# One buffer per slot: the scheduler's choice of a slot carried into the program

## Chip, cores, metric

The kernel runs on one core of a Trainium2 chip. The metric is the device time of one execution in microseconds (us), here the median of three runs. Beside it stands one profiled execution, from which every row below is taken.

## What is computed

The reference is an attention over 32 learned memory slots followed by two feed-forward layers, all in fp32 (8 batches, 8 heads, 576 tokens of 64; 4608 tokens of 512 in the layers, inner width 2048):

```python
a = softmax(phi, over the sequence)
k_m = einsum('bhsm,bhsd->bhmd', a, k);  v_m = einsum('bhsm,bhsd->bhmd', a, v)
attn = softmax(q @ k_m.T / sqrt(64))
x = (attn @ v_m), heads side by side          # 4608 x 512
h = relu(x @ w_in);  x = (s * h * h + b) @ w_out
h = x @ w1;          out = (h * sigmoid(1.702 * h)) @ w2
```

## The kernel before

The work has four stages, each bound to TensorE (PE). In the first, eight batches go through the attention, and `v_m` is multiplied into `w_in`, so that one product gives `h`. The other three are the products with `w_out`, `w1` and `w2` (called `wo`, `w1`, `w2`), each in 6 blocks of 768 tokens. These three use the scheme of Strassen's kind with sums and differences of quarter matrices (tiles named A, B, C, D, E, r). Each fp32 operand is split into a high part `oh` and a low part `ol` (`od` holds both parts of a half tile): ScalarE (ACT) or VectorE (DVE) casts the high part (`hi`, line 276 or 277) and DVE subtracts it (`lo`, line 282). Three matmuls then stand for one product: high by weight-high, low by weight-high, high by weight-low (lines 1217, 1218, 1219 in the last stage). Results in PSUM (X, Y, Z) leave by copies on ACT (`u`, `c`, `a`, line 1236) and additions on DVE. Tiles of the intermediate results lie in HBM and are loaded by transfers that SyncE (SP) issues (line 266).

In the last stage some products of one block belong to another block's output as well. Their sum leaves PSUM as a tile `z` (ACT, line 1346 or 1343), and GpSimd (POOL) issues a transfer that adds it to the output in HBM (`onto`, line 271). The tile's place in SBUF stays taken until that transfer has landed.

The program order of every engine comes from a scheduler written in Python, the class `Order`. Each operation is handed to it with a due time, the tiles it reads and writes, and a cost for each engine that could do it; `sort()` then plays the operations through in modelled time. A tile takes a slot of its tag (`BUFS`: 30 for "w", 33 for "t", 4 for PSUM "ps", 2 for "km", 4 for "nm" and "sm"). The scheduler keeps, for each tag, a heap `free` of the modelled times at which its slots come free, gives a new tile the earliest of them, and puts a slot back at the end of its last user plus 0.2. In that model an engine's result counts as done a little after its operation, a transfer by SP 3.0 after it, and an adding transfer 8.0 after it:

```python
END_LAG = {"sync": 3.0, "acc": 8.0, "dve": 0.09, "act": 0.09}
```

What `sort()` hands on is the order of operations only. When the program is then written in that order, `Net.t` asks a pool of the framework for each tile, with the tag and its number of slots; the pool gives one of the tag's slots whose users all stand earlier in the program, and the first instruction on the new tile waits until the last of those users has ended, or, for a transfer, has landed.

Of the kernel before, what the change touches and what calls it, by code (L numbers as in the profile page):

```python
# [27 lines left out]
class Order:  # L28
# [15 lines left out]
    def __init__(self, bufs):  # L44
        self.bufs, self.ops, self.rank, self.fill, self.until, self.since = bufs, [], [], None, 0, 0
        self.narrow = set()
        self.wrote, self.read, self.users = {}, {}, {}

    def add(self, due, ways, r=(), w=(), first=0):
# [19 lines left out]
    def sort(self):  # L69
        ops, rank = self.ops, self.rank  # L70
        left = [len(o[2]) for o in ops]
        after = [[] for _ in ops]
        tiles = {}
        for n, (due, _, deps, new) in enumerate(ops):
            for d in deps:
                after[d].append(n)
            for x in new:
                tiles.setdefault(x[0], []).append((due, n, x))
        queue = {tag: [x for _, _, x in sorted(v, key=lambda e: e[:2])] for tag, v in tiles.items()}
        free = {tag: [0.0] * n for tag, n in self.bufs.items()}  # L80
        uses = {x: len(v) for x, v in self.users.items()}
        last = dict.fromkeys(uses, 0.0)
        at, end, on, out = {}, [0.0] * len(ops), [None] * len(ops), []
        of = [[] for _ in ops]
        for x, v in self.users.items():
            for n in v:
                of[n].append(x)
        run = False
        held = {"dve": 0.0, "pool": 0.0}
        ready = sorted((rank[n], n) for n in range(len(ops)) if not left[n])  # L90
        since = {n: 0.0 for _, n in ready}
        while ready:
            can = {}
            limit = ready[0][0] + self.AHEAD
            for due, n in ready:
                if due > limit and can:
                    break
                _, ways, deps, new = ops[n]
                t0 = 0.0
                if new:  # L100
                    ok = True
                    for tag in {x[0] for x in new}:
                        mine = [x for x in new if x[0] == tag]
                        f = free[tag]
                        if len(f) < len(mine) or any(x not in queue[tag][:len(f)] for x in mine):
                            ok = False
                            break
                        t0 = max(t0, f[0] if len(mine) == 1 else heapq.nsmallest(len(mine), f)[-1])
                    if not ok:
                        continue  # L110
                best = None
                for i, (eng, cost, _, port) in enumerate(ways):
                    t = max(t0, at.get(eng, 0.0))
                    if port:
                        t = max(t, held["dve" if eng == "pool" else "pool"])
                    for d in deps:
                        e = end[d] + (self.LAG[eng] if on[d] != eng else 0.05)
                        if e > t:
                            t = e
                    score = t + cost * self.WEIGHT.get(eng, 1.0)  # L120
                    if best is None or score < best[0]:
                        best = score, t, eng, i
                can.setdefault(best[2], []).append((best[1], due, n, best[3]))
            if not can:
                raise RuntimeError("no order")
            first = []
            for tag, v in can.items():
                t0 = min(v)[0]
                like = [c for c in v if c[0] <= t0 + 0.1 and c[2] in self.narrow and c[1] >= self.since] if tag == "pe" and run else ()
                if like:  # L130
                    c = min(like, key=lambda c: c[1:])
                    if c[1] < min(v, key=lambda c: c[1:])[1] + self.NEAR:
                        first.append(c)
                        continue
                first.append(min((c for c in v if c[0] <= t0 + (self.SLACK if c[1] < self.until else 0.0)), key=lambda c: c[1:]))
            t, _, n, i = min(first)
            _, ways, _, new = ops[n]
            eng, cost, fn, port = ways[i]
            if port:
                held[eng] = t + cost  # L140
            if self.fill and eng == "pe":
                out.append(lambda n=int((t - at.get(eng, 0.0)) * self.FILL): self.fill and self.fill(n))
            for x in new:
                queue[x[0]].remove(x)
                heapq.heappop(free[x[0]])
            at[eng], on[n] = t + cost, eng
            end[n] = t + cost + self.END_LAG.get(eng, 0.0)
            ready.remove((rank[n], n))
            if eng == "pe":
                run = n in self.narrow  # L150
            out.append(fn)
            for m in after[n]:
                left[m] -= 1
                if not left[m]:
                    bisect.insort(ready, (rank[m], m))
            for x in of[n]:
                last[x] = max(last[x], end[n])
                uses[x] -= 1
                if not uses[x]:
                    heapq.heappush(free[x[0]], last[x] + 0.2)  # L160
        self.span = max(end)
        self.end, self.on = end, on
        return out


class Net:
# [50 lines left out]
    def t(self, k, shape, dt=F32):  # L217

        self.n += 1
        pool = self.ps if k[0] == "ps" else self.sb  # L220
        x = pool.tile(shape, dt, tag=k[0], bufs=self.BUFS[k[0]], name=f"{self.name(k)}_{self.n}")
        self.T[k] = x
        return x

# [1313 lines left out]
```

## Time and profile before

| | |
|---|---|
| time, median of 3 runs | 1376.75 us (1376.53 to 1376.81) |
| the profiled execution, its time | 1375.49 us |
| its span, first to last instruction | 1373.7 us |
| mean granted TensorE clock, as a share of full speed | 0.991 |
| PE busy, share of the span | 1342.7 us, 98% |
| DVE busy | 1130.5 us, 82% |
| ACT busy | 851.4 us, 62% |

An engine is busy while one of its instructions runs. "Idle before" an instruction is the time since the one before it on its engine ended, and the profile names the instruction or transfer whose end released it. An idle time with the releaser "issue" is one for which the profile shows no releaser. Of the profiled execution 1.8 us lie outside the span.

### The profile page before, as it was taken

What the parts mean: (1) busy time and instruction counts of PE and PEld (TensorE: products, weight loads), DVE (VectorE), ACT (ScalarE), POOL (GpSimd) and SP (SyncE); (2) the same over time, 40 slices, a digit from 0 to 9 for tenths busy, and PEclk for the clock granted to TensorE, in tenths of its full rate; (3) what the DMA queues carried; (4) which work ended last, traced back from release to release, by engine and by line L of the source; (5) the groups of instructions that cost most, each with busy time, mean ns of one, the idle gap of its engine ahead of it and who ended that gap; (6) DMA issues with size and microseconds to landing.
All of it is one profiled execution on the core that took longest, in us unless ns stands there. A gap on an engine that the chain in (4) does not pass through costs nothing.

```text
span 1373.7 us, 24220 instructions
## 1 busy us (share of the span) xinstructions
PE 1342.7 (98%) x9088; PEld 1296.6 (94%) x9088; DVE 1130.5 (82%) x1634; ACT 851.4 (62%) x1194; POOL 78.1 (6%) x71
## 2 busy tenths in 40 slices
PE   7999999999999999999999999999999998989898
PEld 6888888899999999999999999999999998989898
DVE  6878996998979988998885997784587786888785
ACT  5766666888877777886564765664454354544443
POOL 2201220200000000000000000000000010101011
PEclk8999999999999999999999999999999999999999
DMA  9989999797865765799999699799898574867673
GB/s 366 364 308 344 341 353 322 263 320 246 303 183 186 245 222 160 248 347 367 349 355 336 259 326 345 272 345 351 316 354 297 192 206 151 225 192 214 216 209 79
DMA packets 149766, 380.49 MB, mean 277 GB/s; under 512 B 16656, under 2 KB 27536, under 8 KB 149648
## 3 DMA queue, kind: packets, MB, share of 16 engines
q1 hardware_dynamic: 145472, 373.24, 77.4%
q0 software_dynamic: 4176, 5.70, 3.1%
q8 instruction: 71, 1.16, 0.4%
q14 instruction: 47, 0.39, 0.1%
HBM read 232.41 MB, written 146.47 MB: 276 GB/s over the span
## 4 chain that ended last, share of the span: by engine, by line
PE 83%; issue 6%; DVE 4%; DMA 4%; ACT 3%; POOL 0%; SPq 0%; ACTq 0%; DVEq 0%; POOLq 0%
PE X L935 5%; PE X L933 5%; PE X L934 5%; PE h L306 5%; PE X L1081 5%; PE X L1083 5%; PE X L1082 5%; PE h L308 4%; PE h L307 4%; PE X L1218 3%; PE X L1219 3%; PE X L1217 3%; PE Y L935 2%; PE Y L933 2%; PE Y L934 2%
## 5 line engine op out<-in xcount | busy, mean ns | idle before, releaser
L306 PE MATMUL h<-ah,mh 128*128 128x288 f32 x512 | 154.9, 302 | 0.3
L308 PE MATMUL h<-ah,ml 128*128 128x288 f32 x512 | 151.0, 295 | 0.2 <-ACT ml L816 0.2
L307 PE MATMUL h<-al,mh 128*128 128x288 f32 x512 | 150.8, 295 | 0.0
L282 DVE TENSOR_TENSOR ol<-A,oh 128x768 fp32r<-128x768 f32 x120 | 113.3, 954 | 33.7 <-ACT oh L276 18.2
L276 ACT CAST oh<-A 128x768 fp32r<-128x768 f32 x111 | 94.5, 866 | 72.7 <-issue 24.6
L1081 PE MATMUL X<-oh,w 128*128 128x384 f32 x384 | 128.6, 335 | 1.2 <-ACT u L1093 0.7
L935 PE MATMUL X<-oh,wo 128*128 128x384 f32 x384 | 128.3, 334 | 0.0
L934 PE MATMUL X<-ol,wo 128*128 128x384 f32 x384 | 128.3, 334 | 0.0
L1082 PE MATMUL X<-ol,w 128*128 128x384 f32 x384 | 128.3, 334 | 0.0
L1083 PE MATMUL X<-oh,w 128*128 128x384 f32 x384 | 128.3, 334 | 0.0
L933 PE MATMUL X<-oh,wo 128*128 128x384 f32 x384 | 128.3, 334 | 0.0
L835 ACT ACTIVATE r<-h 128x576 f32<-128x576 f32 x123 | 86.4, 705 | 59.5 <-PE h L308 50.1
L1217 PE MATMUL X<-oh,w 128*128 128x384 f32 x320 | 110.1, 344 | 8.1 <-ACT u L1236 4.9
L1219 PE MATMUL X<-oh,w 128*128 128x384 f32 x320 | 109.5, 342 | 0.0
L306 PEld LDWEIGHTS h<-ah,mh 128*128 128x128 f32 x512 | 96.1, 188 | 12.3 <-issue 4.5
L1218 PE MATMUL X<-ol,w 128*128 128x384 f32 x288 | 99.2, 344 | 5.4 <-DVE ol L282 5.4
L308 PEld LDWEIGHTS h<-ah,ml 128*128 128x128 f32 x512 | 96.1, 188 | 0.4 <-ACT ml L816 0.4
L307 PEld LDWEIGHTS h<-al,mh 128*128 128x128 f32 x512 | 96.1, 188 | 0.2
L276 ACT CAST oh<-B 128x768 fp32r<-128x768 f32 x70 | 58.9, 856 | 45.6 <-DVE ol L282 18.6
L271 POOL DMA_DIRECT2D out<-z x29 | 25.7, 992 | 1079.7 <-DVE z L282 913.1
L276 ACT CAST oh<-C 128x768 fp32r<-128x768 f32 x68 | 58.7, 879 | 34.7 <-DVE C L282 12.3
L282 DVE TENSOR_TENSOR ol<-B,oh 128x768 fp32r<-128x768 f32 x72 | 67.6, 953 | 12.3 <-DMA out<-z 8.7
(293 smaller groups left out, 3891.6 us busy)
## 6 DMA issues: line engine op xcount, KB each, us to landing
w<-w SPq DMA_DIRECT2D x132, 512.0 KB, 5.8
r<-r SPq DMA_DIRECT2D x128, 288.0 KB, 4.5
kv<-in_kv SPq DMA_DIRECT2D x72, 258.0 KB, 5.4
g<-u SPq DMA_DIRECT2D x48, 384.0 KB, 4.7
raw<-in_w SPq DMA_DIRECT2D x32, 512.0 KB, 6.1
q<-in_q SPq DMA_DIRECT2D x32, 288.0 KB, 5.5
A<-r SPq DMA_DIRECT2D x24, 384.0 KB, 4.8
B<-r SPq DMA_DIRECT2D x24, 384.0 KB, 4.9
```

The lines of the kernel that those rows point to most:

```text
L276: self.order.add(due, [self.act(n, lambda: nc.scalar.copy(out(), src()), psum), self.dve(n, lambda: nc.vector.tensor_copy(out(), src()), f ...
L282: self.order.add(due, [self.dve(n, lambda: nc.vector.tensor_tensor(out(), a(), b(), op=op), port=port)], r, w, first)
L306: self.nc.tensor.matmul(ps, wh, xh, start=start and i == 0, stop=False)
L307: self.nc.tensor.matmul(ps, wh, xl, start=False, stop=False)
L308: self.nc.tensor.matmul(ps, wl, xh, start=False, stop=(i == n - 1))
L933: nc.tensor.matmul(out, T[w][:, 0, c], T[h][:, p], start=f, stop=False, skip_group_check=True)
L934: nc.tensor.matmul(out, T[w][:, 0, c], T[l][:, p], start=False, stop=False, skip_group_check=True)
L935: nc.tensor.matmul(out, T[w][:, 1, c], T[h][:, p], start=False, stop=last, skip_group_check=True)
L1081: nc.tensor.matmul(out, T[w][:, 0, c], T[h][:, k], start=f, stop=False, skip_group_check=True)
L1082: nc.tensor.matmul(out, T[w][:, 0, c], T[l][:, k], start=False, stop=False, skip_group_check=True)
L1083: nc.tensor.matmul(out, T[w][:, 1, c], T[h][:, k], start=False, stop=k == 1, skip_group_check=True)
L1217: nc.tensor.matmul(out, T[w][:, 0, c], T[h][:, p], start=f, stop=False, skip_group_check=True)
```

## The change

The scheduler's heap now holds pairs of a time and the number of a slot. When a tile takes its slot, the number is kept in `slot`, and it goes back into the heap with the slot's next time. `Net.t` asks the pool no longer for "one of 33 slots of tag t" but for the only slot of a tag named after the letter and the number, "t17" say. So the slot that the scheduler chose is the one that the program uses.

```diff
--- before.py
+++ after.py
@@ -44,6 +44,7 @@
     def __init__(self, bufs):
         self.bufs, self.ops, self.rank, self.fill, self.until, self.since = bufs, [], [], None, 0, 0
         self.narrow = set()
+        self.slot = {}
         self.wrote, self.read, self.users = {}, {}, {}
 
     def add(self, due, ways, r=(), w=(), first=0):
@@ -77,7 +78,7 @@
             for x in new:
                 tiles.setdefault(x[0], []).append((due, n, x))
         queue = {tag: [x for _, _, x in sorted(v, key=lambda e: e[:2])] for tag, v in tiles.items()}
-        free = {tag: [0.0] * n for tag, n in self.bufs.items()}
+        free = {tag: [(0.0, i) for i in range(n)] for tag, n in self.bufs.items()}
         uses = {x: len(v) for x, v in self.users.items()}
         last = dict.fromkeys(uses, 0.0)
         at, end, on, out = {}, [0.0] * len(ops), [None] * len(ops), []
@@ -105,7 +106,7 @@
                         if len(f) < len(mine) or any(x not in queue[tag][:len(f)] for x in mine):
                             ok = False
                             break
-                        t0 = max(t0, f[0] if len(mine) == 1 else heapq.nsmallest(len(mine), f)[-1])
+                        t0 = max(t0, f[0][0] if len(mine) == 1 else heapq.nsmallest(len(mine), f)[-1][0])
                     if not ok:
                         continue
                 best = None
@@ -142,7 +143,7 @@
                 out.append(lambda n=int((t - at.get(eng, 0.0)) * self.FILL): self.fill and self.fill(n))
             for x in new:
                 queue[x[0]].remove(x)
-                heapq.heappop(free[x[0]])
+                self.slot[x] = heapq.heappop(free[x[0]])[1]
             at[eng], on[n] = t + cost, eng
             end[n] = t + cost + self.END_LAG.get(eng, 0.0)
             ready.remove((rank[n], n))
@@ -157,7 +158,7 @@
                 last[x] = max(last[x], end[n])
                 uses[x] -= 1
                 if not uses[x]:
-                    heapq.heappush(free[x[0]], last[x] + 0.2)
+                    heapq.heappush(free[x[0]], (last[x] + 0.2, self.slot[x]))
         self.span = max(end)
         self.end, self.on = end, on
         return out
@@ -218,7 +219,7 @@
 
         self.n += 1
         pool = self.ps if k[0] == "ps" else self.sb
-        x = pool.tile(shape, dt, tag=k[0], bufs=self.BUFS[k[0]], name=f"{self.name(k)}_{self.n}")
+        x = pool.tile(shape, dt, tag=f"{k[0]}{self.order.slot[k[:2]]}", bufs=1, name=f"{self.name(k)}_{self.n}")
         self.T[k] = x
         return x
```

The order of instructions is the same on all five engines, tile for tile (8064 rows of PE, 1636 of DVE, 1196 of ACT and 998 of SP). What differs is which earlier tile lay in a tile's slot, and with it the addresses and the waits: 1055 of the 2386 tiles follow another tile than before. Three places show it. In these rows the last number in a name is the tile's own, and behind each instruction stand the counters it waits for: `DMAHW` counts transfers issued from SP, `DMASW` those issued from POOL, `Activation`, `DVE` and `PE` count those engines' instructions.

The first place is ACT in the last stage, where the fourth block begins (z tiles 2023 and 2046 are copied out here). Before:

```order
L1346 COPY z2_2023_12750<-Z2_1894_11977 128x768 [waits PE_49]
L276 CAST oh_2029_12786<-B_1980_12526 128x768 [waits DVE_49,PE_49]
L276 CAST oh_2032_12798<-B_1984_12541 128x768 [waits DVE_49]
L1236 COPY u2_2033_12812<-X_1964_12413 128x768 [waits PE_49]
L276 CAST oh_2034_12815<-B_1993_12585 128x768
L276 CAST oh_2037_12837<-C_2022_12747 128x768 [waits DMAHW7_49,PE_49]
L276 CAST oh_2039_12846<-C_2026_12767 128x768 [waits DMAHW0_49,DVE_49]
L276 CAST oh_2042_12864<-C_2028_12772 128x768 [waits DMAHW1_49,PE_49]
L276 CAST oh_2043_12867<-C_2030_12791 128x768 [waits DMAHW4_49,DMAHW2_49]
L276 CAST oh_2045_12875<-A_2035_12821 128x768 [waits DMAHW3_49,PE_49]
L1346 COPY z2_2046_12890<-Z2_1894_11977 128x384 [waits PE_49]
L276 CAST oh_2052_12927<-A_2038_12840 128x768 [waits DMAHW4_49,DMASW6_49,Activation_49]
```

and after the change:

```order
L1347 COPY z2_2023_12750<-Z2_1894_11977 128x768 [waits DMASW3_49,DMASW2_49]
L277 CAST oh_2029_12786<-B_1980_12526 128x768 [waits DVE_49,PE_49,Activation_49]
L277 CAST oh_2032_12798<-B_1984_12541 128x768 [waits DVE_49,PE_49,Activation_49]
L1237 COPY u2_2033_12812<-X_1964_12413 128x768 [waits PE_49]
L277 CAST oh_2034_12815<-B_1993_12585 128x768 [waits DVE_49]
L277 CAST oh_2037_12837<-C_2022_12747 128x768 [waits DMAHW7_49,PE_49]
L277 CAST oh_2039_12846<-C_2026_12767 128x768 [waits DMAHW0_49,PE_49]
L277 CAST oh_2042_12864<-C_2028_12772 128x768 [waits DMAHW4_49,DMAHW1_49,PE_49]
L277 CAST oh_2043_12867<-C_2030_12791 128x768 [waits DMAHW2_49,DVE_49,Activation_49]
L277 CAST oh_2045_12875<-A_2035_12821 128x768 [waits DMAHW5_49,DMAHW3_49,PE_49]
L1347 COPY z2_2046_12890<-Z2_1894_11977 128x384 [waits DMASW5_49,DMASW4_49,PE_49]
L277 CAST oh_2052_12927<-A_2038_12840 128x768 [waits DMAHW4_49,PE_49]
```

The cast `oh_2052` waited for a transfer of POOL, because it took the slot of `z2_2046` (both lie at byte 128224 of a partition); now it lies where `ol_2031` was, and waits for PE, while `z2_2046` takes the slot of `z2_2023`. The cast `oh_2032` took the slot of `B_1980` before, whose last reader is the DVE instruction that writes `ol_2031`; now it takes that of `oh_2011`, which PE reads last.

The second place is DVE beside it, with the subtraction that writes `ol_2031`. Before:

```order
L282 TENSOR_TENSOR ol_2024_12752<-B_1993_12585,oh_2020_12730 128x768 [waits PE_49,Activation_49]
L282 TENSOR_TENSOR ol_2027_12769<-B_1977_12513,oh_2021_12745 128x768 [waits PE_49,Activation_49]
L282 TENSOR_TENSOR B_1993_12585<-D_2019_12728,A_1946_12290 128x768 [waits DMAHW6_49,DVE_49]
L282 TENSOR_TENSOR A_1930_12192<-C_2022_12747,A_1930_12192 128x768 [waits DMAHW7_49]
L282 TENSOR_TENSOR ol_2031_12796<-B_1980_12526,oh_2029_12786 128x768 [waits DMASW5_49,DMASW4_49,Activation_49]
L282 TENSOR_TENSOR A_1934_12213<-C_2026_12767,A_1934_12213 128x768 [waits DMAHW0_49]
```

and now:

```order
L283 TENSOR_TENSOR ol_2024_12752<-B_1993_12585,oh_2020_12730 128x768 [waits DMAHW5_49,Activation_49]
L283 TENSOR_TENSOR ol_2027_12769<-B_1977_12513,oh_2021_12745 128x768 [waits PE_49,Activation_49]
L283 TENSOR_TENSOR B_1993_12585<-D_2019_12728,A_1946_12290 128x768 [waits DMAHW6_49,DVE_49]
L283 TENSOR_TENSOR A_1930_12192<-C_2022_12747,A_1930_12192 128x768 [waits DMAHW7_49]
L283 TENSOR_TENSOR ol_2031_12796<-B_1980_12526,oh_2029_12786 128x768 [waits PE_49,Activation_49]
L283 TENSOR_TENSOR A_1934_12213<-C_2026_12767,A_1934_12213 128x768 [waits DMAHW0_49]
```

`ol_2031` took the slot of `z2_2023` before and now takes one that PE reads last (`ol_2013`); `ol_2024` now follows a tile that a transfer of SP stores.

The third place is SP at the same point of the program, with the loads of the next block's tiles A. Before:

```order
L266 DMA C_2028_12772<-g_2_2_1_0_9713 128x768 [waits DMAHW1_49,DVE_49]
L266 DMA C_2030_12791<-g_2_3_1_0_9868 128x768 [waits DMAHW2_49,PE_49]
L266 DMA A_2035_12821<-g_3_0_0_0_10036 128x768 [waits DMAHW3_49,PE_49]
L266 DMA A_2038_12840<-g_3_1_0_0_10174 128x768 [waits DMAHW4_49,PE_49]
L266 DMA A_2041_12862<-g_3_2_0_0_10305 128x768 [waits PE_49]
L266 DMA r3_2044_12873<-g_1_0_1_1_8713 128x768 [waits DMAHW6_49,DVE_49,Activation_49]
L266 DMA A_2048_12894<-g_3_3_0_0_10457 128x768 [waits DMAHW7_49,PE_49]
```

and now:

```order
L267 DMA C_2028_12772<-g_2_2_1_0_9713 128x768 [waits DMAHW1_49,DVE_49]
L267 DMA C_2030_12791<-g_2_3_1_0_9868 128x768 [waits DMAHW2_49,PE_49]
L267 DMA A_2035_12821<-g_3_0_0_0_10036 128x768 [waits DMAHW3_49,PE_49]
L267 DMA A_2038_12840<-g_3_1_0_0_10174 128x768 [waits DMAHW4_49,DVE_49]
L267 DMA A_2041_12862<-g_3_2_0_0_10305 128x768 [waits DMAHW5_49,PE_49]
L267 DMA r3_2044_12873<-g_1_0_1_1_8713 128x768 [waits DMAHW6_49,PE_49]
L267 DMA A_2048_12894<-g_3_3_0_0_10457 128x768 [waits DMAHW7_49,PE_49]
```

The load of `A_2038` waited for PE and now waits for DVE, since it takes the slot of `B_1984`, whose last reader is the subtraction that writes `ol_2036`. The loads behind it on SP start after it.

## Rows read from the trace of the kernel before

**Rows 1.** The page's part 1: busy time, share of the span, instructions.

```profile
span 1373.7 us, 24220 instructions
...
PE 1342.7 (98%) x9088; PEld 1296.6 (94%) x9088; DVE 1130.5 (82%) x1634; ACT 851.4 (62%) x1194; POOL 78.1 (6%) x71
```

**Rows 2.** Windows of the second and the last stage: length, busy time of each engine.

```profile
core 0: us, PE busy (x) PEld busy (x) DVE busy (x) ACT busy (x) POOL busy (x), PEclk, DMA share, GB/s
343.00:694.00 351.00, 351.00 (x2027) 351.00 (x2026) 316.43 (x422) 263.60 (x354) 0.00 (x0) 1.00 0.77 264
1030.00:1373.70 343.70, 323.34 (x1811) 319.04 (x1809) 265.51 (x353) 159.11 (x219) 25.71 (x29) 0.98 0.66 198
```

**Rows 3.** PE's waits: instruction and releaser; us in total, times, longest.

```profile
PE X L1218 <- DVE ol L282: 5.4, 5, 2.4
PE X L1217 <- ACT u L1236: 4.9, 2, 4.0
...
PE X L1081 <- ACT u L1093: 0.7, 1, 0.7
```

**Rows 4.** Windows of PE alone around its stalls and at the low clock.

```profile
1139.80:1156.00 16.20, 11.61 (x52) 0.89 0.51 155
1148.90:1152.30 3.40, 3.40 (x13) 0.50 0.98 274
1216.00:1220.20 4.20, 0.24 (x2) 1.00 0.01 4
1220.60:1224.00 3.40, 3.40 (x12) 0.50 0.51 200
1269.80:1279.70 9.90, 5.22 (x26) 0.94 0.87 273
1278.60:1285.40 6.80, 6.49 (x19) 0.50 0.15 40
1317.60:1345.00 27.40, 24.00 (x135) 1.00 0.54 150
```

**Rows 5.** ACT in order of time at the first stall: start, duration, [idle before].

```profile
1139.28 0.83 ACT L276 CAST oh<-B 128x768 fp32r<-128x768 f32 x1 [8.31 <-DVE ol L282]
1140.02 0.79 ACT L1236 COPY u<-X 128x768 f32<-128x768 f32 x1
...
1145.12 0.47 ACT L1346 COPY z<-Z 128x384 f32<-128x384 f32 x1
1153.80 1.56 ACT L276 CAST oh<-A 128x768 fp32r<-128x768 f32 x2 [8.21 <-issue]
```

**Rows 6.** DVE in order of time at the first stall.

```profile
1138.29 0.96 DVE L282 TENSOR_TENSOR ol<-B,oh 128x768 fp32r<-128x768 f32 x1 [4.49 <-DMA out<-z]
...
1140.90 0.95 DVE L282 TENSOR_TENSOR ol<-B,oh 128x768 fp32r<-128x768 f32 x1
```

**Rows 7.** ACT's waits over the whole span: us in total, times, longest.

```profile
ACT oh L276 <- issue: 24.6, 3, 8.3
```

**Rows 8.** Line 271, the adding transfers: who waited, and issue to landing.

```profile
  DVE ol L282: 13.0, 5
...
DMA to landing us min/median/max: 3.5/5.3/8.6
```

**Rows 9.** POOL in order of time at the first stall.

```profile
1145.94 0.86 POOL L271 DMA_DIRECT2D out<-z  x1 [13.59 <-ACT z L1346]
```

**Rows 10.** PE in order of time, two matmuls that release slots.

```profile
1131.25 0.33 PE L1219 MATMUL X<-oh,w 128*128 128x384 f32 x1
...
1200.01 0.33 PE L1218 MATMUL Y<-ol,w 128*128 128x384 f32 x1
```

**Rows 11.** SP's issues, ACT and DVE in order of time ahead of the second stall.

```profile
1203.07 0.32 SPq L266 DMA_DIRECT2D C<-g  x1
...
1212.39 0.96 DVE L282 TENSOR_TENSOR A<-C,A 128x768 f32<-128x768 f32 x1 [3.11 <-DMA C<-g]
...
1212.95 0.83 ACT L276 CAST oh<-A 128x768 fp32r<-128x768 f32 x1 [8.06 <-issue]
```

**Rows 12.** SP's issues at the first stall.

```profile
1133.02 4.11 SPq L266 DMA_DIRECT2D A<-g  x3
```

## The prediction

> **What bounds the kernel now.** I read the page's shares first: PE is busy for 98% of the span, and no other engine is above 82% [rows 1]. Then the windows by stage. The second stage has no idle PE at all, while in the last stage PE is busy for 323.34 of 343.70 us, so 20.36 us are idle there [rows 2]. Of these, 3.7 us lie behind the last matmul, and the change doesn't touch them; the rest is idle time between matmuls. Third, PE's waits: nearly all of it is the first matmul on an operand or on X, which waits for a low part from DVE or for a copy from ACT [rows 3]. Fourth, windows around these waits give the sizes by difference of length and busy time [rows 4]: 4.59 us at 1139.8 to 1156, 3.96 at 1216, 4.68 at 1269.8 to 1279.7, and 3.40 at 1317.6 to 1345, in all 16.63. Behind the first three of them the granted clock is 0.50 of full speed, the 1.2 GHz level instead of 2.4, for 3.40, 3.40 and 6.49 us of busy PE [rows 4]. At half speed that time does half the work, so it costs 6.65 us more. Behind the waits that add up to 3.40 the clock stays at 1.00. So stalls and their clock cost 23.3 us; the rest of the span is PE at full speed.
>
> **Why ACT and DVE are late there.** In the first stall a DVE subtraction `ol` stands idle for 4.49 us until an adding transfer `out<-z` has landed [rows 6]. Its inputs have nothing to do with z: it has the slot that z left. The next cast on ACT idles 8.31 us until that subtraction ends, because its slot is that of the tile read there, and the copy `u`, for which PE waits, stands right behind the cast in ACT's queue [rows 5]. Then ACT idles another 8.21 us, with no releaser named: the cast `oh<-A` at 1153.80. The order rows say what it is: this cast waits for a transfer of POOL, and it has the slot of the z copied at 1145.12 [rows 5], whose transfer POOL issued at 1145.94 [rows 9]; at the 8.6 us that the slowest of these takes to land [rows 8], 1154.5, at the 7.8 that the cast's start implies, 1153.7. Three casts on ACT idle this way for 24.6 us together [rows 7], and DVE idles 13.0 for the same transfers [rows 8]. The pool knew only that the instruction that issues the transfer stands earlier in the program.
>
> **The change, part by part.**
>
> *Instructions.* None is added, removed or moved on any engine, so no busy time changes; the term is 0. What changes is what a tile's first instruction waits for.
>
> *The z slots.* They now go to tiles that come much later. At the first stall `z` itself, at 1145.12 [rows 5], takes the slot whose transfer had landed before the subtraction at 1138.29 began [rows 6], 6.8 us before. Matching the addresses of the built program with the trace, the 17 tiles that follow a z start 5 to 13 us after its landing, where before 16 of 17 started as it landed. The cast of 1139.28 gets a slot whose last reader is the matmul of 1131.25, done at 1131.58 [rows 10]: it could run about 7.7 us earlier, and `u` right behind it, long before PE wants it at 1139.9.
>
> *First stall, 4.59 us.* `u` and both casts leave the path. Next late is the low part of the first tile A, which DVE reaches after the sums that wait for loads C. Those loads wait for DVE's earlier subtractions, which no longer stand behind z, so I take them 2 to 4 us earlier, where 1.9 is needed (the longest of the waits for a low part is 2.4 [rows 3]). Remainder 0.3, with bounds 0 and 1.6.
>
> *Second stall, 3.96 us.* The cast that idled 8.06 us at 1212.95 is free of z [rows 11]. But behind it `u` also waits for DVE, which at 1212.39 had itself waited 3.11 us for a load C [rows 11]. That group of loads begins at 1203.07 [rows 11], when DVE gives its slot back; the new slot is released by a matmul that ends at 1200.34 [rows 10], 2.7 us sooner. The loads then share the transfer engines with the same traffic, so I pass on 2.0 of the 2.7. Remainder 2.0, bounds 0 and 3.96.
>
> *Third stall, 4.68 us.* The same pattern as the first, one pair of blocks later; the cast that idled is the third of the three in [rows 7]. Remainder 0.3, bounds 0 and 1.6.
>
> *The small ones, 3.40 us.* The loads C of the last block also stand behind z slots on SP. I leave 0.6, bounds 0 and 3.4.
>
> *The clock, 6.65 us.* The waits at 1317.6 to 1345 (3.40 us, the longest 2.24) were followed by no fall [rows 4], so a remainder of 2.0 should cause none: I take back all of it; the bound below is one fall left, 3.4 us at half speed, 1.7.
>
> *The third stage.* One wait for `u`, 0.7 us [rows 3]: ACT's copy waits there for a slot that PE reads; its new slot is free earlier. Gain 0.7.
>
> *New waits.* Some tiles now follow a tile that is released later than they start today. The largest is the load of the second A at the first stall: SP issued it within the group that begins at 1133.02 [rows 12]; now it waits for the subtraction that runs from 1140.90 to 1141.85 [rows 6], some 7 us later, with all later loads of SP behind it. That subtraction is itself late because of the 8.31 us. Its tile is cast at 1153.80 [rows 5] today, and with its load 7 us later it would still be there at about 1148.4. I put all new waits together at 2.0 us, bounds 0 and 6 (two such places, each at most the 3 us by which the load could miss PE, as PE arrives some 5 us sooner).
>
> **The sum.** Stalls 16.63 − 0.3 − 2.0 − 0.3 − 0.6 = 13.43; clock 6.65; third stage 0.7; new waits −2.0; in all 18.8 us. The profiled execution took 1375.49 us, 1.3 below the median of 1376.75; taken off the median, this gives **1358.0**. All bounds favourable: 16.63 + 6.65 + 0.7 = 24.0, so 1352.8. All unfavourable: 16.63 − 1.6 − 3.96 − 1.6 − 3.4 = 6.1, clock 6.65 − 1.7 = 4.9, third stage 0.7, new waits −6, in all 5.7, so 1371; they won't all fall together.
>
> **Rivals.**
>
> *The waits only move.* The tag has 33 slots as before, and if they are too few, another tile waits instead. For it: two thirds of the last stage's tiles change their slot, and loads on SP now wait for DVE or PE. By it stalls 1 and 3 would keep half of their length and the second all: the gain is about 2.3 + 0 + 2.3 + 2 of stalls and half of the clock, 3.3, some 10 us, so 1367; in the full form 1376. Against it: a slot that was free 7.7 us earlier stood beside the one that was given. The Trainium skill (Perfetto Trace Analysis, Optimization Strategy) says that a gap that repeats on the engine that should be saturated can mean too little SBUF for the next tile; by that rule alone the choice of a slot gives nothing and the time is 1376. The trace speaks for a wrong slot rather than for too few.
>
> *Slower.* In the second stage DVE is busy for 316.43 of 351.00 us [rows 2], and PE has no slack. Some 30 of the operand tiles there now wait for PE's last reading of another tile. If such waits added more than 34.6 us to DVE's queue, DVE would become the bound and each further us would be PE's; to undo the 18.8 they would have to reach 53. Set against today's starts, they add a few us. At 60 the time would be 1383.
>
> *Nothing happens.* The waits go but PE is held by the loads anyway: 1374 to 1377. Against it stands that no load is PE's releaser in the last stage [rows 3].
>
> **How the numbers follow.** Forecast, 1352.8 to 1363: 0.74. Waits move in part, 1363 to 1371: 0.15. No change within 0.2% (2.8 us, about what a measurement of this kernel can tell from none), by loads that hold PE or by waits that move in full: 0.06. Slower: 0.05. So faster 0.89, same 0.06, slower 0.05. The range 1352.5 to 1367 holds the forecast and more than half of the second case, some 0.82.
>
> **What would show it.** PE busy in the last stage over 95% of a shorter window; no 0.50 of the clock after the first 35 us, or one stretch of it; no idle of 8 us before a cast `oh`, no `out<-z` as a releaser for DVE or ACT; `u` at the second stall still some 2 us late, with a load C as the root. The prediction is wrong if PE's idle time comes back behind the loads A of SP, or if the first three stages, which have hardly any idle PE now, show some.

## The result, and the profile after

The changed kernel took **1358.95 us** in the median of 4 executions (1358.38 to 1360.28), the kernel before 1376.64 beside it; the ratio is 0.9878 (0.9861 to 0.9895). The forecast was 1358.0. The total came out; several terms of the sum did not, and their errors happened to cancel.

Page part 1 of the changed kernel, as in [rows 1]:

```profile
span 1357.2 us, 24177 instructions
...
PE 1341.2 (99%) x9088; PEld 1299.6 (96%) x9088; DVE 1132.8 (83%) x1634; ACT 857.8 (63%) x1194; POOL 77.9 (6%) x71
```

Its windows of the second stage and of the last, the columns as in [rows 2]:

```profile
343.00:694.00 351.00, 351.00 (x2008) 351.00 (x2007) 314.42 (x416) 262.37 (x351) 0.00 (x0) 1.00 0.77 259
1030.00:1357.20 327.20, 322.45 (x1840) 321.47 (x1838) 271.09 (x359) 164.56 (x221) 25.66 (x29) 1.00 0.71 214
```

PE's waits from 1030 us on, as in [rows 3]; this is the only one:

```profile
PE X L1219 <- DVE D L283: 0.3, 1, 0.3
```

In the last stage PE idles 0.35 us between matmuls instead of 16.6, and the granted clock is 1.00. No cast idles 8 us any more (the longest wait of one is 7.4, for a matmul; before, such a wait reached 7.3 too). Where [rows 7] had 24.6 us in three waits of up to 8.3, the same line now reads:

```profile
ACT oh L277 <- issue: 14.1, 9, 2.9
```

ACT in order of time where the first stall was, as in [rows 5]:

```profile
1137.83 0.83 ACT L277 CAST oh<-B 128x768 fp32r<-128x768 f32 x1 [1.24 <-PE X L1220]
1138.57 0.79 ACT L1237 COPY u<-X 128x768 f32<-128x768 f32 x1
...
1146.73 0.47 ACT L1347 COPY z<-Z 128x384 f32<-128x384 f32 x1
1150.21 0.83 ACT L277 CAST oh<-A 128x768 fp32r<-128x768 f32 x1 [3.01 <-PE X L1219]
```

The cast ahead of `u` waits for PE now, and the cast behind z for a matmul, not for z's transfer. So far this is what was forecast.

**What doesn't fit** stands in the second stage. PE is busy for all of its 351.00 us at clock 1.00 in both kernels, but it starts 2008 matmuls there, where before it started 2027 [rows 2]. The 19 missing ones are 3.3 us. Matched matmul by matmul, the changed kernel falls further and further behind, by 6.1 us at 1120 us, and then gains 23.2 in the last stage. The mean of one matmul in 380 to 640 us shows it too; in the changed kernel:

```profile
L936 PE MATMUL X<-oh,wo 128*128 128x384 f32 x280 | 94.3, 337 | 0.0
```

The same group in the kernel before:

```profile
L935 PE MATMUL X<-oh,wo 128*128 128x384 f32 x281 | 93.9, 334 | 0.0
```

From the start of one matmul to the start of the next (a step, below) it is 173.3 ns before, with hardly any variation (173 to 174), and 175.0 after, between 168 and 185. With 2008 + 1923 + 1840 = 5,771 matmuls from 343 us on, 1.6 to 1.7 ns each are 9 to 10 us. The runs below ask first where this comes from, then whether z was the cause of the stalls.

### The profile page after: what moved, and what is told of

Its sections match the earlier page's. It is cut to its first block, busy times and chain, and to the rows that moved or that the text cites. A ratio compares the mean times of both kernels' runs of the same rounds, so it can differ in the third digit from the quotient of the medians.

```text
span 1357.2 us, 24177 instructions
## 1 busy us (share of the span) xinstructions
PE 1341.2 (99%) x9088; PEld 1299.6 (96%) x9088; DVE 1132.8 (83%) x1634; ACT 857.8 (63%) x1194; POOL 77.9 (6%) x71
## 4 chain that ended last, share of the span: by engine, by line
PE 92%; DVE 5%; DMA 1%; ACT 1%; issue 1%; SPq 0%; DVEq 0%; ACTq 0%
PE X L934 5%; PE X L936 5%; PE X L1083 5%; PE X L1082 5%; PE X L935 5%; PE X L1084 5%; PE h L307 4%; PE h L309 4%; PE h L308 4%; PE X L1219 4%; PE X L1220 4%; PE X L1218 4%; PE Y L1082 2%; PE Y L936 2%; PE Y L1084 2%; PE Y L934 2%
## 5 line engine op out<-in xcount | busy, mean ns | idle before, releaser
L1380 ACT ACTIVATE u<-u 128x768 f32<-128x768 f32 x48 | 40.7, 847 | 51.2 <-DVE u L283 51.2
```

## Experiments

In the diffs, w and t are the tags of the large tiles: w for weights, t for the split operands and everything else. All kernels issue the same instructions in the same order on every engine; what differs is the slots and their addresses, and with them the waits. The kernel before took 1373.0 to 1373.7 us in the median beside these runs.

### The pace of PE: chip, choice of slots, or addresses

The two kernels unaltered, on one chip.

> The changed kernel, unaltered, a second time. In its first trace the matmuls of the last three stages start 174.9 ns apart on the mean (168 to 185), where those of the kernel before start 173.3 apart, without variation; by instruction the changed kernel falls some 6 us behind before it gains 23 in the last stage. Theory one (the new choice of slots itself slows PE's stepping, through addresses in SBUF or banks of PSUM): the steps are 174.5 to 175.5 again and the time is 1358 to 1360. Theory two (it was the chip or that one execution): the steps are 173.3 in this trace, or the time falls to 1352 to 1354 in some executions.

> The kernel before, unaltered, profiled on the same chip. If the steps belong to the kernel: 173.3 ns between matmuls of the second stage and 1373 to 1377 us. If they belong to the chip: 174.9 ns, and 1380 us or more.

Measured: 1358.89 us (1358.10 to 1360.38) with steps of 175.0 ns, and 1371.20 (one execution) with 173.3. The pace belongs to the kernel.

In the built programs the pool laid w and t in two blocks; with one tag for each slot the slots stand in order of first use, and the small tiles nm, km and sm (32 to 1024 bytes) come to lie between them. The next kernel claims w and t ahead:

```diff
-        for fn in self.order.sort():
+        fns = self.order.sort()
+        for tag, n in (("w", 512), ("t", 384)):
+            for i in range(self.BUFS[tag]):
+                self.sb.tile([P, 2, n], F32, tag=f"{tag}{i}", bufs=1, name=f"first_{tag}{i}")
+        for fn in fns:
             fn()
```

> The changed kernel with the same choice of slots, but the 30 slots of w and the 33 of t are claimed in order before the first instruction, so that the two kinds lie in two blocks of SBUF as in the kernel before, instead of interleaved by first use. No wait changes. If the interleaved addresses slow PE's stepping: steps of 173.3 ns, 1352 to 1353.5 us. If they don't: 174.9 ns and 1358 to 1360 us.

Measured: **1349.70 us** (1349.22 to 1350.33), steps of 173.3 to 173.4 ns, 2026 matmuls in the second stage's window:

```profile
343.00:694.00 351.00, 351.00 (x2026) 350.84 (x2025) 316.58 (x422) 263.86 (x354) 0.00 (x0) 1.00 0.78 263
```

The gain is larger than the expected 1352 to 1353.5 allowed for. So the addresses cost the change 9.2 us. Which property of them? A kernel with the carried slot for t alone gave the hint.

```diff
+        one = k[0] in ('t',)
+        tag, bufs = (f"{k[0]}{self.order.slot[k[:2]]}", 1) if one else (k[0], self.BUFS[k[0]])
-        x = pool.tile(shape, dt, tag=f"{k[0]}{self.order.slot[k[:2]]}", bufs=1, name=f"{self.name(k)}_{self.n}")
+        x = pool.tile(shape, dt, tag=tag, bufs=bufs, name=f"{self.name(k)}_{self.n}")
```

> Only the tiles of kind t get the scheduler's slot; w, km, nm, sm and the PSUM tiles stay in the pool's rotation, and w and t lie in two blocks. Theory z (the stalls of the last stage come from t tiles put behind an adding transfer): no idle of 8 us before a cast, no idle PE over 1 us in the last stage, and 1352 to 1360 us by what the steps are (173.3 or 174.9). Rival (the choice for w or PSUM brings part of the gain): at least one of the four stalls of 3.4 to 4.7 us comes back, 1362 to 1368 us.

Measured: 1358.20 us (1357.81 to 1359.15), 0.06 us of idle PE from 1030 to 1330 us, steps of 174.7 to 175.0 ns. So t alone brings the whole gain; the slots of w and PSUM bring none that can be measured. And two blocks are not enough. Here the small tiles lie between t's. Its matmuls from 350 to 1340 us, sorted by the start addresses of the moving operand (t) and of the weights of the matmul behind it (w), each as the remainder of 256 bytes (60 more have the weights at 96):

```
moving   weights   matmuls   mean step
  224      224       3581     173.4 ns
   96      224       2009     177.4 ns
```

Three kernels test the remainder. One (aligned) leaves w and t interleaved, but claims the small tiles first, so that all begin at one remainder. Two put 128 unused bytes ahead of a block (t_shift128 ahead of t, all_shift128 ahead of both). Below stand the line of aligned and the added lines of t_shift128; in all_shift128 the tag asked for is w:

```diff
+        for tag, n in (("nm", 8), ("km", 256), ("sm", 24)):
...
+            if tag == "t":
+                self.sb.tile([P, 32], F32, tag="pad", bufs=1, name="pad")
```

> The changed kernel, with w and t slots interleaved by first use as there, but the small slots (nm, km, sm) claimed before them, so that every w and t slot begins at the same remainder of 512 bytes (224). In the changed kernel the remainders are mixed. In the kernel with only t carried, the steps sorted by the first operand's address gave 173.4 ns at the remainder 224, that of the weights, and 177.3 at 352. Theory remainder: steps of 173.3 ns and 1349 to 1351 us, as with the two blocks. Theory blocks (w and t must lie apart): 174.9 ns and 1358 to 1360.

> The version with two blocks, with 128 unused bytes between them: w slots stay at remainder 224 of 512 bytes, every t slot is at 352. No wait changes. Theory remainder: every matmul of the last three stages reads its moving operand at 352 and its weights at 224, steps of 175.9 ns (what such neighbours have in the kernel with only t carried) to 177.3, on some 5,800 matmuls 15 to 23 us more than the two blocks: 1364 to 1373. Theory blocks: 173.3 and 1349 to 1351.

> The version with two blocks, with 128 unused bytes ahead of both: all w and t slots are at remainder 352. If it is the agreement of the two operands that counts: 173.3 ns and 1349 to 1351 us. If it is the remainder of the moving operand alone: 175.9 to 177.3 ns and 1364 to 1373, as with t alone shifted.

Measured: aligned 1349.43 us (1348.56 to 1349.87), t alone shifted 1365.45 (1365.02 to 1365.98), both shifted 1349.91 (1348.52 to 1350.57). The second stage's window, of these three in this order:

```profile
343.00:694.00 351.00, 351.00 (x2026) 351.00 (x2026) 316.56 (x423) 264.60 (x354) 0.00 (x0) 1.00 0.77 263
```

```profile
343.00:694.00 351.00, 351.00 (x1996) 351.00 (x1995) 312.82 (x414) 261.80 (x351) 0.00 (x0) 1.00 0.76 258
```

```profile
343.00:694.00 351.00, 351.00 (x2027) 351.00 (x2026) 316.42 (x422) 263.67 (x354) 0.00 (x0) 1.00 0.77 263
```

What matters is the count behind PE's busy time: 2026, 1996, 2027, with the same 351.00 us busy. Interleaving costs nothing; where all operands begin at one remainder, the loss is gone. With t at 96 and w at 224 the steps are 176.0 ns, and 2.7 ns on 5,771 matmuls are 15.6 us, as measured (15.7). Matmul by matmul the changed kernel doesn't follow so simple a rule: the 1183 steps whose two operands agree in the remainder of 256 bytes take 174.7 ns there, the other 4466 take 175.1. That agreement gives the pace is shown for kernels in which (nearly) all matmuls agree, not for single ones among others.

One more, with 256 bytes in place of 128 between the blocks:

> The version with two blocks, with 256 unused bytes between them: w slots at remainder 224 of 512 bytes, t slots at 480; remainders of 256 bytes agree, those of 512 don't. If agreement at 256 bytes is enough: 173.3 ns and 1349 to 1351 us. If it takes 512: 175.9 ns and 1364 to 1367, as with 128.

Measured: 1350.03 us (1348.93 to 1350.64), 173.3 ns. Agreement in the remainder of 256 bytes is enough; that of 512 isn't needed.

### The stalls: is it z?

These kernels have the two blocks, so 1349.70 is their base. In the first (z_blind), the choice of a slot counts z's slot as free when its transfer is issued, and doesn't know when it lands:

```diff
+                issued[x] = max(issued.get(x, 0.0), t + cost if eng == "acc" else end[n])
...
+                    heapq.heappush(slots[x[0]], (issued[x] + 0.2, self.slot[x]))
```

> The version with two blocks, same order of instructions, but where a slot is chosen, a tile that an adding transfer reads counts as free when that transfer is issued, not 8 us later; every other tile counts as before. Theory z (the stalls were t tiles put behind an adding transfer that had not landed): waits of casts for z's transfer come back, idle PE in the last stage of 10 us or more and part of the clock's 6.65: 1362 to 1373 us. Rival (any choice by the scheduler's times cures the stalls, z or not): 1349 to 1351.

Measured: 1356.16 us (1354.19 to 1358.21), 6.5 more than the base; 5.5 us of idle PE from 1030 to 1330 us and one stretch at half clock:

```profile
1030.00:1330.00 300.00, 294.53 (x1686) 293.36 (x1685) 255.00 (x340) 155.95 (x212) 22.13 (x25) 0.99 0.72 220
1288.00:1295.00 7.00, 5.97 (x25) 5.97 (x26) 3.67 (x5) 4.67 (x6) 1.76 (x2) 0.76 0.88 232
```

Neither theory's number was hit: z's part comes back, but it is smaller here than before. In the next two (fifo, fifo_z) the choice knows no times and takes the slot whose last instruction stands earliest in the program; in the second a slot with z in it comes into that order only when the scheduler's time has reached the landing (the lines are fifo_z's; fifo has the last one alone):

```diff
+                    if x in adds:
+                        heapq.heappush(flying, (last[x] + 0.2, x))
+                    else:
+                        heapq.heappush(slots[x[0]], (len(out), self.slot[x]))
```

> The version with two blocks and the same order of instructions, but each tile takes the slot whose last instruction stands earliest in the program, without any time of the scheduler. That is close to what the pool does in the kernel before. Theory order (a choice that knows no times gives the stalls): they come back, 10 to 20 us of idle PE in the last stage and clock behind them, 1362 to 1376 us. If the pool's stalls come from a detail of its own: 1350 to 1358.

> As the kernel with the order of the program alone, but a slot whose last reader is an adding transfer comes into the order only when the scheduler's time has reached the landing (8 us). Theory z (the transfers are what the order of the program doesn't see): within 2 us of the choice by times, 1349 to 1352. Rival (with z's known, the choice by order of the program still puts tiles behind others that are released late, as the 6.5 us that z alone cost lets expect): at least a third of the loss of the order of the program stays, 1355 to 1368.

Measured: 1358.87 us (1357.34 to 1362.21), between the two expectations, and **1350.94** (1349.28 to 1352.51), as theory z expected. PE's waits from 1030 us on, by program order alone:

```profile
PE X L1233 <- DVE ol L297: 3.6, 3, 2.6
PE Z L1343 <- ACT z L1361: 1.9, 1, 1.9
PE X L1233 <- DVE D L297: 0.6, 1, 0.6
```

and with z held back:

```profile
PE X L1236 <- DVE D L300: 1.5, 1, 1.5
PE Z L1346 <- ACT z L1364: 0.2, 1, 0.2
```

Knowing the landing of z's transfers and nothing else takes 7.9 of the 9.2 us that program order costs; the times of all other tiles are worth 1.2, within the spread of the runs.

The last kernel starts from the kernel before, with its own slots and addresses; the t slots stand in a table, in which z's followers (the next tiles in their slots) are exchanged.

```diff
+            tag, bufs, self.nt = f"t{int(self.SLOTS[self.nt], 36)}", 1, self.nt + 1
```

> The kernel before with its own layout and its own slots for w, PSUM and the small tiles; the slots of the t tiles are written out as a table of what the pool gave, and altered only in the last stage: a tile that would follow a z before z's transfer has landed is exchanged with a slot that stands free at that place in the program (70 exchanges, 68 t tiles with another predecessor, all behind z's; before them the t slots are the pool's). Theory z (the z followers alone make the four stalls): all stalls of over 1 us go, as does the half clock in the last stage, and the gain is that of the whole change without its loss in PE's stepping, 22 to 24 us, to within 2 us of the two blocks: 1349 to 1352. Rival (what z costs is a third, as the choice by times that is blind to z alone lets expect, 6.5 of 23; the rest is spread over other tiles): one of the stalls of 3.4 us or more stays, 1356 to 1368.

The table that ran has 57 exchanges, not 70. It was worked out in the order in which the kernel before lists its instructions, and at six places there no other t slot is free; z keeps its follower at these, and they include both z's of the first stall and both of the third. (Sixteen tiles, most of them weights, follow another tile too, all ahead of the last stage.) Measured: 1363.65 us (1356.83 to 1366.71; 1360.56 in the profiled execution). That is not theory z's 1349 to 1352 but within the rival's range, and the first and third stall stay; since they are those without an exchange, the run can't tell theory z from the rival there. Windows around the first, second and third stall and the small ones:

```profile
1139.80:1156.00 16.20, 11.23 (x61) 10.07 (x60) 9.93 (x14) 7.49 (x12) 0.86 (x1) 1.00 0.48 150
1205.00:1222.00 17.00, 17.00 (x100) 16.83 (x99) 15.00 (x25) 8.68 (x14) 0.86 (x1) 1.00 0.68 207
1262.00:1275.00 13.00, 10.59 (x58) 9.69 (x58) 7.89 (x14) 2.87 (x5) 0.52 (x1) 1.00 0.72 220
1315.00:1345.00 30.00, 29.75 (x171) 29.23 (x171) 26.40 (x40) 15.64 (x22) 1.77 (x2) 1.00 0.38 105
```

Its cast behind z in the first stall, as in [rows 5]:

```profile
1153.11 1.56 ACT L300 CAST oh<-A 128x768 fp32r<-128x768 f32 x2 [8.22 <-issue]
```

The kernel before, profiled again, has these windows in its last stage, around the same four places:

```profile
1139.80:1156.00 16.20, 12.03 (x54) 10.72 (x54) 9.64 (x13) 7.50 (x12) 0.86 (x1) 0.89 0.47 148
1212.00:1222.00 10.00, 6.62 (x33) 6.31 (x32) 8.73 (x15) 5.22 (x9) 0.00 (x0) 0.89 0.29 116
1265.00:1275.00 10.00, 7.45 (x33) 6.88 (x33) 6.74 (x9) 3.84 (x6) 0.89 (x1) 0.80 0.56 164
1310.00:1345.00 35.00, 32.32 (x185) 31.62 (x184) 29.60 (x45) 17.74 (x27) 2.65 (x3) 1.00 0.59 183
```

So in one kernel: where z's follower was exchanged, the idle PE goes from 3.38 to 0 and from 2.68 to 0.25; where it was not, it stays, 4.17 to 4.97 and 2.55 to 2.41. The table with all 70 wasn't run, so that z alone makes the whole of the pool's loss is shown for the second stall and the small ones, not for the first and third. Counted over the kernels, of the 17 tiles behind a z in its slot:

```
kernel            start within 0.35 us of the landing   time
before                          16                      1373.0 to 1376.6
exchanged table                 11                      1363.65
program order                   14                      1358.87
blind to z                      14                      1356.16
program order, z held            0                      1350.94
two blocks                       0                      1349.70
```

## Why the prediction was right, and the step that failed

**Instructions, "the term is 0": wrong, by some 9.2 us.** No instruction was added or moved, and yet each matmul kept PE longer: a mean of 337 ns instead of 334 in its record, and steps of 175.0 ns instead of 173.3, by the new addresses. (PE's busy sum of the whole span hides this, 1341.2 against 1342.7 us, because the half clock went at the same time.) The prediction saw that addresses change only as a matter of which tile follows which. Shown by the same slots at other addresses: 1358.9 against 1349.4 to 1350.0.

**z slots: right.** The followers start 2.7 to 12 us behind the landing in the changed kernel (forecast 5 to 13), and the waits behind z are gone.

**Remainders, 0.3 + 2.0 + 0.3 + 0.6: too large.** 0.35 us is left in all. At the second stall the 2 us behind a load C did not show; the whole of the 3.96 went, not half.

**The stalls themselves: too small.** A matmul counts as busy for 334 ns, but the next one starts after 173. A gap in PE's busy time thus hides another 0.16 us. From start to start, the 12 gaps of the last stage lose 19.15 us (each step less 173.3 ns), where the idle time is 16.63.

**The clock, 6.65: right that all of it goes, too large in size.** No half clock is left behind 35 us. The last stage gave back 25.1 us between the traces of before and of the two blocks, whose pace is the same; gaps and slow matmuls together make up 24.2 of these when counted by starts. Less the 19.15 of the gaps that leaves the half clock about 5 us: 35 steps of 0.32 us in place of 0.173. The forecast took half of the 13.29 us of busy time there; some of that time lies in steps that are counted with the gaps here.

**Third stage, 0.7: too small, 2.1** by the same two traces.

**New waits, −2.0: none.** The load of the second A (the second of the three in [rows 12]) does wait for the subtraction as forecast. Its issue in the kernel before, in the changed kernel behind the subtraction that releases it, and in the kernel with two blocks:

```profile
1134.73 0.32 SPq L266 DMA_DIRECT2D A<-g  x1
```

```profile
1141.42 0.95 DVE L283 TENSOR_TENSOR ol<-B,oh 128x768 fp32r<-128x768 f32 x1
...
1142.40 0.32 SPq L267 DMA_DIRECT2D A<-g  x1
```

```profile
1134.65 0.32 SPq L267 DMA_DIRECT2D A<-g  x1
```

By the clock it is 7.7 us later in the changed kernel, but 6.2 of these are the lost pace, by which everything there is late; with the same slots and the pace restored it isn't later at all. A's cast at 1150.21 waited 3.01 us for a matmul, not for the load. The forecast itself noted that this subtraction was late only because of the 8.31 us; freed of that, its new successor costs nothing.

So 25.1 + 2.1 = 27.2 us came back, the pace took some 9.6, and the start of the program was 0.4 slower: 17.2 are left at the last matmul, where 18.8 were forecast. (The spans differ by 16.5, as 0.6 us more lie behind the last matmul.) The errors, 8.4 too little gained and 9.6 of loss not seen, cancelled. That the total came out within 1 us is luck; the mechanism of the stalls is not. The all-favourable bound, 1352.8, was no bound: with the addresses in order the same choice of slots gives 1349.7.

**The rivals.** "The waits only move" is refuted: 33 slots are enough. The cause that the Trainium skill (Perfetto Trace Analysis, Optimization Strategy) says a repeating gap can have, too little SBUF for the next tile, is not the one in this trace: the gap was a matter of which slot, 0.35 us of it being left with the same number. "Slower": DVE is busy for 314.42 of 351.00 us in the second stage and has no part in the loss; PE itself lost time there, by a way that the rival did not have. "Nothing happens": no load holds PE.

**Open.** Program order costs 9.2 us, the pool's own choice 23.3 to 24. In the programs the four z's of the first and third stall are followed two tiles earlier by the pool (z 2023 by tile 2031 instead of 2033, z 2046 by 2052 instead of 2054), at casts and parts that PE needs at once. That this makes the difference is argued, not shown. So what is shown of z is: carrying the slots of t alone removes all stalls; in a choice by program order, z's landing is worth 7.9 of 9.2 us; and in the kernel before, exchanging z's followers alone removes the second stall and the small ones. That z alone makes its first and third stall rests on the waits in its trace ([rows 6] and [rows 7]).

## What to carry to other kernels

Where a tile is the source of a transfer that only writes memory, look who gets its slot next: a pool that goes by program order gives it out while the transfer is still under way, and the wait lands on whatever stands there in an engine's queue. Where a change moves addresses, don't book 0 for the instructions: compare the count of matmuls in a window in which PE is busy throughout, since the busy share can't show a slower pace. Claim tags of odd sizes apart from the operand tiles, so that moving tiles and weights begin at the same remainder of 256 bytes; here that made the best version, 1349.4 to 1350.0 us, 1.8% under the kernel before (ratio 0.9826, 0.9811 to 0.9841).

## What the runs showed of the hardware

The pace of a matmul of 128x384 in fp32r depended on where its operands begin in SBUF: 173.3 ns from start to start where moving operand and weights throughout have the same remainder of 256 bytes (both 224, both 96), 176.0 with the moving operand at 96 and the weights at 224, 175.0 on the mean where remainders were mixed. (The 177.4 above are such matmuls in between others.) Where remainders were mixed, agreement of a single pair explained little (174.7 against 175.1), so the rule for single matmuls is not known. Differences of 32 or 64 bytes weren't tried alone, nor other shapes and types, and why it is so stays open. The Trainium skill (SBUF — State Buffer, Operand start alignment) asks only that an operand begin at a multiple of its element size, and says that this is about what is legal, not about speed. All these addresses are multiples of 32 and legal; the speed differed by 1.5%.

In the kernel before, a stretch of half clock followed the first stall with its 4.59 us of idle PE [rows 4]. In the exchanged table PE was idle there for 4.97 us, the longest single wait 2.4, and the clock stayed at 1.00.
